# Stack loads over four rounds, output weights in five loads, packing from GpSimd's queue

## The chip, the cores and the metric

The kernel runs on one core of one Trainium2 chip. The metric is the device time of one execution in microseconds; the figure given is the median of several runs. A profile is one further execution, recorded by the hardware profiler.

## The reference

Four layers follow each other on `x` (2048 tokens, 576 features): A, B, A, B, each with a layer norm in front and a residual around it. A is attention with a sliding window of 256 and 32 heads of 18 features; B filters in the frequency domain.

```
def A(x):                       # D = 576, H = 32, Dh = 18, W = 256
    q, k, v = split(x @ wqkv)
    scores = q @ k.T * Dh ** -0.5, masked to 0 <= i - j < W
    return merge(softmax(scores) @ v) @ wo
def B(x):                       # two dimensions, tokens and features
    return irfft2(rfft2(x) * (w_r + 1j * w_i))
x = x + A(layernorm(x)); x = x + B(layernorm(x))
x = x + A(layernorm(x)); x = x + B(layernorm(x))
```

## The kernel before

`prompt_kernel` builds two pairs of an attention layer (`layer_a`) and a spectral layer (`layer_b`); the output projection of the attention, the class `Out`, lies between them. The change touches the attention's main part and `Out`.

**Heads, chunks and rounds.** The 32 heads are worked on in `NQ` = 8 groups of four. A group's sequence is 16 tiles of 128 tokens, in four chunks of 512. The running number x = 16 n + i counts tiles over all groups, 128 in all; a *round* is one x. A round has four score products of each of two kinds, one for each head (`pair`, `hp`):

- `score_max` (L1168, tile S) multiplies queries by keys, and VectorE takes the row maximum (L1170, m). It runs `LEAD` = 10 rounds ahead of the second kind.
- `exps` (L1205, tile E) multiplies keys by queries and a row that holds the negated maximum, so that ScalarE's exponential (L1206, tile P) comes out already shifted. GpSimd sets what lies outside the window to zero (L1208, L1211).
- `part` (L1225, tile U) multiplies P by the values.

**From projection to stacks.** `proj` (L1107) multiplies the normalized tokens by the query and key weights; its result is split in a high and a low part (sg) and stored in DRAM (qk_d, L1128). The low part of later blocks is made by GpSimd (L1125). `stack_load(n, c)` (L1143) fetches chunk c of group n from there into the tiles qs and ks, stacked over partitions as high and low parts: for q and k, for hp 0 and 1, three transfers each, twelve in all, of 72 KB. `qs` and `ks_` have two buffers each, used by groups in turn. `v_load` (L1149 or L1151) fetches a group's values (vq).

**The maxima.** `m_rows(n, c)` turns the maxima of a chunk (L1181), ScalarE negates them (L1183, tile mt), and four transfers of 2 KB (L1188, qs<-mt) write them to the last row of each stack. E of a chunk's tiles needs them; a tile's queries reach two tiles further, so E needs chunk c (c over 0) two rounds before that chunk's own first round.

**Attended values.** After the last `part` of a chunk in burst k, VectorE turns U (L1230), then come `divide` (L1241, L1242) at k + 1, `back` (L1246, tile o) at k + 3 and `store` (L1251, op_d<-o) at k + 4. When a group's four chunks are stored, four calls of `pack(n, h)` (L1258, o_d<-op_d) copy the 18 used rows of 32 of each head from one DRAM tensor to another, in steps 2 bursts apart.

**Order.** The order is written out by hand. `opening` runs the first ten rounds of S. `bursts` then takes three E and three S at a time (a burst is 0.75 round), with products of the projection (up to round 103 or so), parts, and the `steps` put down for that burst. `loads(t)` is called at the start of each round, `behind(t)` at its end. The last ten rounds (`MIX` = 118 on) follow in a loop of their own with two steps a round. Each engine, and each queue that issues transfers (SP, ACT's, POOL's), works in program order; a transfer on SP that waits holds what stands behind it on SP.

**Out.** `room()` runs at round OB - 16 = 104 and asks for the raw output weights (L742) in two transfers; `split(k)` (L749, L750) makes the high and low parts of a fifth of them at rounds 110, 112 to 118. `const` (L756, dc), `load_x` (L764) and `attended` (L772, L775: o_d into oraw) fetch what the output projection (L800, tile ops) and the next layer need. `turn` (L785) and `split_last` (L794) prepare the attended values.

Some copies between DRAM tensors (L1404, dcr<-in_dc and gcr<-in_gc) are issued on GpSimd's queue in the first attention; three pieces of a stack load go there in the opening.

Of the kernel before, what the change touches and what calls it, by code (L numbers as in the profile page):

```python
# [18 lines left out]
NT = 16  # L19
# [622 lines left out]
NQ = 8  # L642
# [73 lines left out]
class Out:  # L716
# [7 lines left out]
    def room(self):  # L724
        self.rh = rh = self.bp.tile([128, 5 * S], F32R, tag="xh", name="oroom")
        self.rl = f = self.bp.tile([128, 4 * S], F32, tag="xl", name="ofree")
        X = 2 * self.n
        self.w = {"h": rh[:, 0:5 * X], "l": rh[:, 5 * X:10 * X]}
        self.oT = [rh[:, 5800 + 896 * k:6696 + 896 * k] for k in range(3)]
        self.oL = [rh[:, 8488 + 256 * k:8744 + 256 * k] for k in range(3)]  # L730
        self.gc = rh[:, 9256:9768].rearrange("p (a j c) -> p a j c", a=2, j=2)
        small = f[:, 8130:8170]
        self.st = [small[:, 12 * k:12 * k + 12] for k in range(2)]
        self.mv = [small[:, 24 + 2 * k:26 + 2 * k] for k in range(4)]
        self.rs = [small[:, 32 + k:33 + k] for k in range(4)]
        self.junk, self.junk2 = f[:, 6804:7092], f[:, 7092:7380]
        self.raw = f[:, 0:5 * X]
        self.x = [f[:, X * k:X * k + X] for k in range(5)]

        self.o7 = f[:, 4756:6804]  # L740
        for a, b in ((0, 2), (2, 5)):
            self.nc.sync.dma_start(self.raw[:, a * X:b * X], self.wo_d[:, a * X:b * X])  # L742

    def xt(self, u):
        return self.x[(u + 4) % 5]
# [118 lines left out]
def layer_a(tc, ident, eps, bp, big, src, dst, wqk_d, wv_d, wo_d, dc_d, gc_d, dram, copy, wvs, second, spectral, share):  # L864

    nc = tc.nc
    V, A, T, P = nc.vector, nc.scalar, nc.tensor, nc.gpsimd
# [14 lines left out]
    if True:  # L882
# [191 lines left out]
        with ExitStack() as c2:  # L1074
# [56 lines left out]

            vts = {}

            def stack_load(n, c):

                q, k = qs[n % 2], ks_[n % 2]
                cs = slice(c * 512, c * 512 + 512)
                for which, t, parts in ((0, q, (0, 0, 1)), (1, k, (0, 1, 0))):
                    for hp in range(2):
                        r0 = 144 * n + 72 * which + 36 * hp  # L1140
                        for slot, part in enumerate(parts):
                            b = 64 * hp + 18 * slot
                            (P if which and (n == 0 and c > 1 or n == 1 and c == 0) else nc.sync).dma_start(  # L1143
                                t[b:b + 18, :, cs].bitcast(F32), qk_d[part, r0:r0 + 36, cs].rearrange("(f d) t -> d f t", f=2).bitcast(F32))

            def v_load(n):
                v = wp.tile([128, NT, 4, 19], F32, tag="vq", name=f"vq{n}", bufs=2)
                if second:
                    nc.sync.dma_start(v.rearrange("p b h e -> p b (h e)"), v_d[n].rearrange("(b p) e -> p b e", p=128))  # L1149
                else:  # L1150
                    nc.sync.dma_start(v.rearrange("p b h e -> p (b h e)"), v_d[n].rearrange("p b e -> p (b e)"))  # L1151
                vts[n] = v
# [102 lines left out]

            def pack(n, h):
                a, b = [f.rearrange("e c x -> (e c x)").rearrange("(a b) -> a b", a=16) for f in (o_d[72 * n + 18 * h:72 * n + 18 * h + 18], op_d[n, 32 * h:32 * h + 18])]
                nc.sync.dma_start(a, b)  # L1258

            for k, (i, c) in enumerate(((0, 0), (1, 0), (0, 1), (1, 1), (0, 2), (0, 3), (1, 2), (1, 3))):  # L1260
                for f in proj(i, c, k % 2):
                    f()
                remainders()

                for b in (32, 96):
                    P.memset(ks_[i][b:b + 32, :, 512 * c:512 * c + 512].bitcast(F32), 1.0)
                    P.memset(qs[i][b:b + 32, :, 512 * c:512 * c + 512].bitcast(F32), 0.0)
                if k in (2, 4):
                    stack_load(0, k // 2 - 1)
# [7 lines left out]
            def loads(t):  # L1277
                if t + LEAD in (0, 2):
                    stack_load(0, 2 + (t + LEAD) // 2)
                if t in (-4, 4, 8, 12):  # L1280
                    stack_load(1, max(t, 0) // 4)
                n, c = divmod(t + 20, NT)
                if c % 4 == 0 and 1 < n < NQ:
                    stack_load(n, c // 4)
                if t + LEAD == 5:
                    v_load(0)
                if t + 12 in range(NT, NX, NT):
                    v_load((t + 12) // NT)
# [18 lines left out]
            steps = {}  # L1307

            def later(k, n, c):
                for lag, f in zip(later.lags, (divide, back, store)):  # L1310
                    steps.setdefault(k + lag, []).append((f, n, c))
                if c == 3:
                    for h in range(4):
                        steps.setdefault(k + (8 + 2 * h if n < NQ - 2 else 7 + h // 2), []).append((pack, n, h))

            later.lags = 1, 3, 4

# [10 lines left out]
            def bursts():  # L1328
# [8 lines left out]
                for k in range(-(-len(es) // 3)):  # L1337
                    e, c = es[3 * k:3 * k + 3], ss[3 * k:3 * k + 3]
                    for x, pair, hp in e:
                        if pair == hp == 0:  # L1340
                            loads(x)
                            assert not any(source(p) == x - 6 for p in parts)
# [9 lines left out]
                    while parts and (took < 430 or source(parts[0]) < e[0][0] - 3 if spread else took == 0 or parts[0][0] % 2 or parts[0][1]):  # L1352
                        if (4 * source(parts[0] if spread else (parts[0][0] | 1, 1)) + 3) // 3 + 2 > k:
                            break
                        x, half = parts[0]
                        if took and half == 0 and (x % 4 == 0 or x % NT == 1):
                            break
                        parts.pop(0)
                        part(x, half)
                        took += lasting((x, half))  # L1360
                        if half and x % 4 == 3:
                            later(k, *divmod(x // 4, 4))
# [24 lines left out]
                    for x, pair, hp in e:  # L1387
                        if pair == hp == 1:
                            behind(x)
                remainders()  # L1390
                assert at == len(pj)
                for p in parts:
                    part(*p)
                    if p[1] and p[0] % 4 == 3:
                        later(k, *divmod(p[0] // 4, 4))

            OB = NX - 8
            out = Out(nc, eps, bp, big, o_d, srcv, dstv, wo_d, dc_d, gc_d, second)

            def behind(t):  # L1400
                if copy and t >= 32 and t % 4 == 0 and t < 32 + 16 * len(copy):

                    z, r = divmod(t // 4 - 8, 4)
                    P.dma_start(*[a[32 * r:32 * r + 32] for a in copy[z]])  # L1404
                if t == OB - 16:
                    out.room()
                if 0 <= t - (OB - 10) < 10 and t % 2 == 0:
                    out.split((t - (OB - 10)) // 2)
                if t - OB + 13 in range(0, 10, 2):
                    out.const((t - OB + 13) // 2)  # L1410
                if t == OB - 3:
                    out.filters()
                if t - OB + 8 in range(0, 10, 2):
                    out.load_x(((t - OB + 8) // 2 + 1) % 5)
                if 0 <= t - (OB - 8) < 6:
                    out.attended(*divmod(t - (OB - 8), 2))
                if t - OB in (1, 2):
                    out.attended(3, t - OB - 1)
                if t == OB + 4:
                    out.ahead_of_last()  # L1420
                if t - OB - 5 in (0, 1, 2):
                    out.turn(t - OB - 5, V)
                if t == NX:

                    A.activation(wp.tile([128, 1], F32, name="se", bufs=1), eps, AF.Sqrt)
# [14 lines left out]
            for t in range(MIX, NX + 2):  # L1440
                loads(t)
                for pair in range(2):
                    for hp in range(2):
                        if t < NX:
                            exps(t, pair, hp)
                    for f, *a in steps.pop(now, ()):
                        f(*a)
                    if pair == 0 and t - 2 < NX:
                        pv(t - 2)
                        if t % 4 == 1 and t - 2 < NX - 4:  # L1450
                            later(now, *divmod(t // 4 - 1, 4))
                    now += 1
                for f, *a in due[:1]:
                    f(*a)
                    due.pop(0)
                behind(t)
# [65 lines left out]
```

## Time and profile before

| | |
|---|---|
| median of 3 runs | 1370.67 us (1363.26 to 1371.69) |
| the profiled execution's own time | 1368.36 us |
| its span, first to last instruction | 1366.3 us |
| mean granted clock of TensorE | 0.988 |
| TensorE busy | 1312.9 us (96%) |
| VectorE, ScalarE, GpSimd busy | 948.7 us (69%), 754.9 us (55%), 696.1 us (51%) |
| bytes moved by DMA | 274.23 MB, 201 GB/s in the mean |

The two attentions' bursts lie at about 128 to 479 us and 829 to 1178 us of the span. In the rows, PE is TensorE's matmuls, PEld its weight loads, DVE VectorE, ACT ScalarE, POOL GpSimd, SP the queue of SyncE; a q behind a name means the sequencer that issues transfers. `out<-in` are the names of tiles. A row of a timeline gives start, duration, engine, line and operation, and in brackets the engine's idle time before it and what ended that. A group's row gives its count, busy time, mean ns of one, and idle time before it with the releasers.

### The profile page before, as it was taken

How to read it: one execution, taken by the hardware profiler on the slowest of the kernel's cores; microseconds unless marked ns; L12 is line 12 of the kernel's file. 1: busy time of each engine (PE TensorE's matmuls, PEld its weight loads, DVE VectorE, ACT ScalarE, POOL GpSimd, SP SyncE). 2: the span in 40 equal slices, each digit the busy share in tenths (PEclk: the TensorE clock that was granted, in tenths of full speed). 3: DMA queues.
4: the chain of work that ended last, by engine and by line, in shares of the span. 5: the costliest groups of instructions: out<-in, count | busy, mean ns of one | idle time of the engine just before them, and what ended most of it. 6: DMA issues, size and time to landing. Idle time of an engine off the chain costs nothing.

```text
span 1366.3 us, 33335 instructions
## 1 busy us (share of the span) xinstructions
PE 1312.9 (96%) x10911; PEld 964.4 (71%) x10911; DVE 948.7 (69%) x3132; ACT 754.9 (55%) x1896; POOL 696.1 (51%) x1156
## 2 busy tenths in 40 slices
PE   9999999899998899999999999999999998999998
PEld 8986666566655499985899975556556654699588
DVE  5418888788887577757674148888788878476755
ACT  5622776577766735443355315677667767575233
POOL 2257666566655634567221295566556657212731
PEclk9999999999999999999999999999999999999999
DMA  6756665666556827678883367566556568488875
GB/s 204 210 165 204 201 200 178 196 189 181 180 173 201 242 78 245 194 244 266 275 264 74 99 202 210 183 183 182 178 176 174 181 173 280 132 288 298 300 246 178
DMA packets 179392, 274.23 MB, mean 201 GB/s; under 512 B 68415, under 2 KB 78399, under 8 KB 177893
## 3 DMA queue, kind: packets, MB, share of 16 engines
q1 hardware_dynamic: 168399, 250.71, 59.4%
q10 hardware_dynamic: 7702, 15.03, 3.1%
q0 software_dynamic: 3120, 6.36, 1.8%
q8 instruction: 88, 1.44, 0.4%
q14 instruction: 83, 0.68, 0.2%
HBM read 164.54 MB, written 114.81 MB: 204 GB/s over the span
## 4 chain that ended last, share of the span: by engine, by line
PE 84%; DMA 7%; DVE 3%; ACT 3%; issue 2%; POOL 1%; SPq 1%; ACTq 0%; DVEq 0%; POOLq 0%
PE pj L1107 19%; PE S L1168 12%; PE U L1225 11%; PE vps L1003 9%; PE ops L800 6%; PE E L1205 6%; DMA qs<-mt 4%; PE po L274 4%; PE pq L524 3%; PE p L503 2%; PE pf L274 2%; PE pi L600 2%; PE pz L312 1%; ACT P L1206 1%; DMA dc<-dcr 1%
## 5 line engine op out<-in xcount | busy, mean ns | idle before, releaser
L1170 DVE CUSTOM_DVE_ANT_0 jk<-S,mask 128x384 bf16<-128x384 f32 (+2 forms) x1024 | 490.0, 526 | 102.7 <-PE S L1168 59.8
L1206 ACT ACTIVATE P<-E 128x384 f32<-128x384 f32 (+2 forms) x1024 | 409.4, 475 | 206.7 <-PE E L1205 172.8
L1168 PE MATMUL S<-ks,qs 63*128 63x384 f32 (+2 forms) x1024 | 282.8, 378 | 2.0 <-DVE m L1170 0.8
L1208 POOL TENSOR_SCALAR_AFFINE_SELECT P<-P 128x512 f32<-128x512 f32 x256 | 163.8, 640 | 235.5 <-ACT P L1206 227.1
L1205 PE MATMUL E<-qs,ks 64*128 64x384 f32 (+2 forms) x1024 | 236.0, 381 | 29.0 <-DMA qs<-mt 22.2
L1168 PEld LDWEIGHTS S<-ks,qs 63*128 63x128 f32 x1024 | 147.0, 187 | 116.5 <-DVE m L1170 81.5
L1225 PE MATMUL U<-P,vq 128*19 128x128 f32 (+1 forms) x3840 | 193.2, 334 | 3.3 <-DVE us L1230 2.2
L1205 PEld LDWEIGHTS E<-qs,ks 64*128 64x128 f32 x1024 | 121.0, 189 | 51.8 <-ACT P L1206 23.4
L1107 PE MATMUL pj<-xh,wqh 128*128 128x512 f32 x360 | 156.3, 434 | 0.4 <-DVE sg L1125 0.2
L1225 PEld LDWEIGHTS U<-P,vq 128*19 128x19 f32 x3840 | 96.7, 99 | 84.5 <-issue 22.4
L1211 POOL TENSOR_SCALAR_AFFINE_SELECT P<-P 128x512 f32<-128x512 f32 x224 | 143.0, 638 | 0.0
L1107 PE MATMUL pj<-xh,wql 128*128 128x512 f32 x360 | 122.9, 418 | 0.0
L1107 PE MATMUL pj<-xl,wqh 128*128 128x512 f32 x288 | 120.1, 417 | 0.0
L800 PE MATMUL ops<-oroom 128*128 128x290 f32 (+1 forms) x812 | 114.0, 297 | 1.7 <-DVE ofree L846 1.3
L800 PEld LDWEIGHTS ops<-oroom 128*128 128x128 f32 x812 | 110.4, 189 | 2.3 <-ACT ofree L834 1.5
L1107 PEld LDWEIGHTS pj<-xh,wqh 128*128 128x128 f32 x360 | 68.0, 189 | 32.5 <-issue 14.4
L1170 DVE DVE_READ_ACCUMULATOR2_ANT m<- 128x1 f32 x1024 | 84.9, 83 | 0.0
L1119 ACT CAST sg<-pj 128x512 fp32r<-128x512 f32 x72 | 42.3, 588 | 70.7 <-PE pj L1107 62.2
L1107 PEld LDWEIGHTS pj<-xh,wql 128*128 128x128 f32 x360 | 64.5, 189 | 21.9 <-issue 10.9
L1230 DVE STREAM_TRANSPOSE us<-U 128x512 f32<-128x512 f32 x64 | 45.8, 716 | 46.4 <-PE U L1225 46.4
L1107 PEld LDWEIGHTS pj<-xl,wqh 128*128 128x128 f32 x288 | 54.5, 189 | 16.9 <-issue 9.0
L274 PE MATMUL po<-dc,half 128*128 128x290 f32 x384 | 63.4, 302 | 0.0
(508 smaller groups left out, 2206.9 us busy)
## 6 DMA issues: line engine op xcount, KB each, us to landing
qk_d<-sg SPq DMA_DIRECT2D x56, 512.0 KB
qs<-qk_d SPq DMA_DIRECT2D x384, 72.0 KB
ks<-qk_d SPq DMA_DIRECT2D x348, 72.0 KB
op_d<-o SPq DMA_DIRECT2D x56, 256.0 KB
v_d<-vt SPq DMA_DIRECT2D x32, 304.0 KB
vq<-v_d SPq DMA_DIRECT2D x16, 608.0 KB
wt<-in_w SPq DMA_DIRECT2D x16, 580.0 KB
ofree<-x SPq DMA_DIRECT2D x16, 580.0 KB
```

The lines of the kernel that those rows point to most:

```text
L274: T.matmul(ps[:, c, 0:NF], tail[r] if si == 4 else hl_(si), dcs[b // 2][r, b % 2], start=mi == si == 0, stop=si == 4)
L800: self.nc.tensor.matmul(self.ps[u][n][:, 0:self.n], x, self.w[p][:, (2 * wk + n) * self.n:(2 * wk + n + 1) * self.n], start=first and i == ...
L1003: T.matmul(ps[:, n, 0:288], xT(xk, c), w[:, wk, n * 288:(n + 1) * 288], start=i == 0, stop=i == len(ks) - 1)
L1107: T.matmul(box["ps"].rearrange("r (n p) -> r n p", n=NT) if second else box["ps"], w[:, wk], x, start=s == 0, stop=s == len(ks) - 1)
L1168: T.matmul(ps[:, 0:N], q[b:b + 63, pair, i * 128:i * 128 + 128], k[b:b + 63, pair, lo:hi], start=True, stop=True)
L1170: V.tensor_tensor_reduce(out=jk[:, 0:N], in0=ps[:, 0:N], in1=mask[:, 384 - N:384], scale=1.0, scalar=-3e38, op0=ALU.add, op1=ALU.max, accu ...
L1205: T.matmul(ps[:, 0:nq], k[b:b + 64, pair, j * 128:j * 128 + 128], q[b:b + 64, pair, j * 128:j * 128 + nq], start=True, stop=True)
L1206: A.activation(p[:, hl_, 0:nq], ps[:, 0:nq], AF.Exp, scale=SC)
L1208: P.affine_select(out=p[:, :, 0:128], in_=p[:, :, 0:128], pattern=[[0, 4], [1, 128]], compare_op=ALU.is_ge, fill=0.0, base=0, channel_mult ...
L1211: P.affine_select(out=p[:, :, 256:384], in_=p[:, :, 256:384], pattern=[[0, 4], [-1, 128]], compare_op=ALU.is_gt, fill=0.0, base=0, channel ...
L1225: T.matmul(U[32 * h:32 * h + 19, (q0 % 4) * 128:(q0 % 4) * 128 + 128 * (q1 - q0)], vts[n][:, j, h], pt[n, j][:, h, (q0 - j) * 128:(q1 - j) ...
L1230: V.transpose(u, U.rearrange("r (p n) -> r n p", n=NT))
```

## The change

Three things change.

- A chunk's twelve transfers are asked for in four rounds, three in each: q for hp 0, q for hp 1, k for hp 0, k for hp 1. They begin in the round in which all twelve stood before. In rounds 12 to 15 the last chunk of group 1 and the first of group 2 are loaded side by side. The first chunk of group 1 (round -4) and group 0 stay as they were.
- The raw output weights come in five transfers, one for each `split`, at rounds 104, 106 to 112.
- `pack` is issued on GpSimd's queue in place of SP, and two steps later: at k + 10, 12, 14, 16 in place of k + 8, 10, 12, 14, and for the last of these groups at k + 9, 9, 10, 10 in place of k + 7, 7, 8, 8.

```diff
@@ class Out, room
         self.o7 = f[:, 4756:6804]
-        for a, b in ((0, 2), (2, 5)):
-            self.nc.sync.dma_start(self.raw[:, a * X:b * X], self.wo_d[:, a * X:b * X])
+
+    def weights(self, k):
+        c = slice(2 * self.n * k, 2 * self.n * (k + 1))
+        self.nc.sync.dma_start(self.raw[:, c], self.wo_d[:, c])
@@ stack_load
-            def stack_load(n, c):
+            def stack_load(n, c, some=range(4)):
 
                 q, k = qs[n % 2], ks_[n % 2]
                 cs = slice(c * 512, c * 512 + 512)
                 for which, t, parts in ((0, q, (0, 0, 1)), (1, k, (0, 1, 0))):
                     for hp in range(2):
+                        if 2 * which + hp not in some:
+                            continue
                         r0 = 144 * n + 72 * which + 36 * hp
@@ pack
-                nc.sync.dma_start(a, b)
+                P.dma_start(a, b)
@@ loads
-                if t in (-4, 4, 8, 12):
-                    stack_load(1, max(t, 0) // 4)
-                n, c = divmod(t + 20, NT)
-                if c % 4 == 0 and 1 < n < NQ:
-                    stack_load(n, c // 4)
+                if t == -4:
+                    stack_load(1, 0)
+                n, c = divmod(t + (12 if t < 16 else 20), NT)
+                if 4 <= t < 16 or 1 < n < NQ and t >= 12:
+                    stack_load(1 if t < 16 else n, t // 4 if t < 16 else c // 4, (t % 4,))
+                if 12 <= t < 16:
+                    stack_load(2, 0, (t % 4,))
@@ later
-                        steps.setdefault(k + (8 + 2 * h if n < NQ - 2 else 7 + h // 2), []).append((pack, n, h))
+                        steps.setdefault(k + (10 + 2 * h if n < NQ - 2 else 9 + h // 2), []).append((pack, n, h))
@@ behind
                 if t == OB - 16:
                     out.room()
+                if t - OB + 16 in range(0, 10, 2):
+                    out.weights((t - OB + 16) // 2)
```

## The prediction

> **What bounds the kernel now.** I read the page first, its busy shares and its chain by line, then the costliest groups.
>
> ```profile
> PE 1312.9 (96%) x10911; PEld 964.4 (71%) x10911; DVE 948.7 (69%) x3132; ACT 754.9 (55%) x1896; POOL 696.1 (51%) x1156
> PE pj L1107 19%; PE S L1168 12%; PE U L1225 11%; PE vps L1003 9%; PE ops L800 6%; PE E L1205 6%; DMA qs<-mt 4%; PE po L274 4%; PE pq L524 3%; PE p L503 2%; PE pf L274 2%; PE pi L600 2%; PE pz L312 1%; ACT P L1206 1%; DMA dc<-dcr 1%
> L1205 PE MATMUL E<-qs,ks 64*128 64x384 f32 (+2 forms) x1024 | 236.0, 381 | 29.0 <-DMA qs<-mt 22.2
> ```
>
> TensorE is busy for 1312.9 of 1366.3 us, so whatever is to be won lies in its 53 us of idle time and in its clock. The largest item with one name is qs<-mt: the small transfers of the negated row maxima (L1188), for which E (L1205) stands idle 22.2 us. They are issued on SP, the queue that the change relieves.
>
> What would a stretch without such waits cost? The view by windows compares two stretches of the first attention that do the same work, sixteen rounds each: the first has none of these waits, the second has the one of the third line.
>
> ```profile
> 306.90:349.40 42.50, 42.31 (x424) 25.93 (x426) 35.71 (x138) 29.43 (x74) 25.28 (x38) 1.00 0.60 181
> 213.70:261.80 48.10, 46.28 (x430) 28.06 (x426) 37.10 (x145) 30.31 (x77) 29.71 (x44) 0.96 0.65 200
> ...
> 244.39 1.14 PE L1205 MATMUL E<-qs,ks 64*128 64x384 f32 x3 [1.79 <-DMA qs<-mt]
> ```
>
> Columns of the first two: stretch, its us, then busy us of PE, PEld, DVE, ACT and POOL, granted clock, DMA. The first shows what is left when no maxima are late: 42.5 us with TensorE busy 42.3, so nothing else stands ready to take the wait's place there. The second is 5.6 us longer, with a wait of 1.8 us and a clock of 0.96. In the whole trace six stretches run near half clock, beside such waits; first, last and sum:
>
> ```profile
> 244.30:247.70 3.40, 3.31 (x10) 1.98 (x10) 1.21 (x5) 1.59 (x4) 0.58 (x1) 0.54 0.43 129
> ...
> 1162.50:1169.30 6.80, 6.64 (x54) 2.94 (x58) 0.00 (x0) 3.63 (x9) 1.40 (x3) 0.52 0.51 143
> sum 30.60, PE 28.90 PEld 14.92 DVE 8.91 ACT 13.03 POOL 8.24; mean PE 4.82 PEld 2.49 DVE 1.49 ACT 2.17 POOL 1.37
> ```
>
> Why are the maxima late? SP's timeline at the worst wait among the bursts, with ScalarE's and TensorE's rows:
>
> ```profile
> 959.60 0.27 ACT L1183 ACTIVATE mt<-tpm 16x128 fp32r<-16x128 f32 x1 [0.42 <-PE tpm L1181]
> 957.70 0.53 SPq L1258 DMA_DIRECT2D o_d<-op_d  x1
> ...
> 958.95 2.44 SPq L1143 DMA_DIRECT2D qs<-qk_d  x6
> 961.44 4.05 SPq L1143 DMA_DIRECT2D ks<-qk_d  x6
> 965.53 0.84 SPq L1258 DMA_DIRECT2D o_d<-op_d  x1
> ...
> 967.09 2.56 SPq L1188 DMA_DIRECT2D qs<-mt  x4
> 969.28 0.41 PE L1205 MATMUL E<-qs,ks 64*128 64x384 f32 x1 [2.76 <-DMA qs<-mt]
> ```
>
> The maxima are ready at 959.87 and leave at 967.09. In those 7.2 us SP works off one stack load, twelve issues in 6.5 us, and one pack. E at 969.28 has waited 2.76 us. So the bound is SP's order, not the transfer: from first issue to E's start it takes 2.2 us.
>
> SP itself stands still too. In the view of waits (who waited for what: us in total, times, longest), E first, then SP:
>
> ```profile
> PE E L1205 <- DMA qs<-mt: 22.2, 13, 3.4
> ...
> SPq L1143 <- DMA qk_d<-sg: 60.7, 35, 9.5
> SPq L1143 <- DMA qs<-qk_d: 32.1, 63, 2.6
> SPq L1258 <- DMA op_d<-o: 20.2, 10, 3.4
> ```
>
> The third line is issues of one stack load that wait for earlier ones to land; the last is the pack at the head of SP, waiting for the store that it reads.
>
> **Part 1, the stack pieces.** Nothing is removed: a chunk still takes 12 issues, now three in each of four rounds. In program order the maxima of chunk c come about 1.3 rounds before the next chunk's first pieces, and the store of the attended values about one round after them. Before, the twelve stand ahead of both. Now six stand ahead of the store, at most six more between store and maxima. Twelve take 4.9 us or more (the 364.77 rows below: 2.14 + 2.73, 0.36 us each at least), so the maxima meet a queue shorter by 2.2 us at least, and by what of the 32.1 us of mutual waits the smaller groups avoid. A wait of 2.76 us with 7.2 us of lag needs 2.8 us. The price is that a chunk's last pieces are asked for three rounds (3 x 42.5/16 = 8 us) later. S (L1168) reads chunks ten rounds ahead of E, and seven rounds, 18.6 us, remain. For head group 1 the load starts only six rounds ahead of its reader, so three rounds are left, and from round 12 to 15 two loads run at once, six issues a round, 2.2 of 2.7 us. There I expect S to wait 1 us or so per attention: 2 us in all; bounds 0 and 6 us (three chunks, 1 us each, two attentions).
>
> **Part 2, packs on POOL.** SP loses 56 issues of 0.53 us, 30 us, and the 20.2 us of waiting. POOL gains the issues. Their nearest row is a copy between DRAM tensors issued from POOL in the same rounds:
>
> ```profile
> L1404 POOL DMA_DIRECT2D dcr<-in_dc x4: 557/572/590, 218.2 to 254.9; - x4
> L1208 POOL TENSOR_SCALAR_AFFINE_SELECT P<-P 128x512 f32<-128x512 f32 x256 | 163.8, 640 | 235.5 <-ACT P L1206 227.1
> L1225 PE MATMUL U<-P,vq 128*19 128x128 f32 (+1 forms) x3840 | 193.2, 334 | 3.3 <-DVE us L1230 2.2
> 372.73 0.64 POOL L1211 TENSOR_SCALAR_AFFINE_SELECT P<-P 128x512 f32<-128x512 f32 x1
> 375.14 1.50 PE L1225 MATMUL U<-P,vq 128*19 128x256 f32 x32
> ```
>
> That is 56 x 0.57 = 32 us on an engine that waits 227 us for ScalarE's exponentials at its masks (L1208). The cover: POOL's last mask ends at 373.37, and the U that could read it starts at 375.14, 1.8 us later; TensorE stands 3.3 us in all before U. So 0.57 us at a time costs nothing; without that cover it would be the whole 32 us.
>
> The change adds a wait on POOL: the first pack of a group waits for the landing of the fourth store, and masks and the remainders of the projections queue behind it. How late is that store?
>
> ```profile
> 361.33 0.71 DVE L1246 STREAM_TRANSPOSE o<-us 128x512 f32<-128x512 f32 x1
> 364.77 2.14 SPq L1143 DMA_DIRECT2D qs<-qk_d  x6
> 366.96 2.73 SPq L1143 DMA_DIRECT2D ks<-qk_d  x6
> 369.78 0.34 SPq L1151 DMA_DIRECT2D vq<-v_d  x1
> 370.22 0.38 SPq L1251 DMA_DIRECT2D op_d<-o  x1
> 377.43 0.53 SPq L1258 DMA_DIRECT2D o_d<-op_d  x1
> ```
>
> Its data are ready at 362.04; it leaves at 370.22, behind twelve stack issues, and the pack follows on its landing at 377.4. With six pieces fewer it leaves 2.2 us earlier, and the packs come two bursts later (a burst is 0.75 round, 2.0 us), 4 us. The longest such wait on SP was 3.4 us, less than 6.2. I take 0. The other bound is that nothing is gained: 14 first packs x (3.4 - 1.8) = 22 us.
>
> **Part 3, the weights, and the end of the attention.**
>
> ```profile
> 429.73 0.86 SPq L742 DMA_DIRECT2D ofree<-in_wo  x2
> 431.22 7.37 DMA qs<-mt
> 438.72 1.03 PE L1205 MATMUL E<-qs,ks 64*128 64x384 f32 x2 [1.55 <-DMA qs<-mt]
> 452.38 0.56 SPq L1251 DMA_DIRECT2D op_d<-o  x1
> 457.01 0.25 ACT L1183 ACTIVATE mt<-tpm 16x128 fp32r<-16x128 f32 x1
> 459.20 1.74 SPq L1258 DMA_DIRECT2D o_d<-op_d  x2
> 461.05 2.88 SPq L1188 DMA_DIRECT2D qs<-mt  x4
> 463.56 1.25 PE L1205 MATMUL E<-qs,ks 64*128 64x384 f32 x2 [2.23 <-DMA qs<-mt]
> 469.40 3.28 SPq L775 DMA_DIRECT2D oraw<-o_d  x4
> ```
>
> The line with 7.37 is from the chain. These maxima take so long because 1.44 MB of weights was asked for just ahead; in five loads, two of 288 KB are. Three more issues of 0.43 us per layer fall on a queue that has lost more. Each load still comes six rounds, over 12 us, before its split. The last maxima are ready at 457.26 and held until 461.05 by a pack that waits for the store of 452.38. Off SP, they leave 3.8 us earlier, and E's 2.23 us go. These packs are now two rounds later; the loads that read them (L775) were issued from 469.4 on, so they stay hidden.
>
> **The sum**, against the profiled execution's 1368.4 us (its span is 1366.3):
> - E's waits: 22.2 us. I keep 4 us for places where large loads still lie ahead of the maxima: -18.
> - Clock: of 30.6 us at half clock, the three stretches of 3.4 us and one of 6.8 us lie where TensorE is the limit; half of 17 is 8.5. The other two lie at an attention's end, where ScalarE limits: 0.5 each. -9.5. Next late after that is TensorE itself, as in the 42.5 us stretch.
> - Late pieces +2, POOL 0.
>
> 1368.4 - 18 - 9.5 + 2 = 1343. The median shown is 1370.7, 2.3 us above that execution; I name 1343 and leave this in the range.
>
> The Trainium skill (TensorE: Matmul & The Clock Gate, What's actually happening) lets the clock drop after an idle window of about 3.4 us. Of E's 13 waits the longest is 3.4 us and the one beside the first slow stretch 1.8, so the trace is stricter than the page; by the page the clock term would stay and the sum be 1352.
>
> **Rivals.**
> 1. *Half.* SP runs ahead of the rounds as far as its waits let it, so the pieces spread in program order may still bunch, and the 60.7 us for qk_d, true dependences, stay. Then packs and weights alone act: the two ends (2.2 + 3.4 + 1), the 1.55 us at 438.72 with its clock 1.7, and perhaps 4 more: 14, 1355. For it: late head groups load what was projected just before. Against: at 958.95 the twelve are held up by nothing but themselves. Chance 0.18.
> 2. *POOL gives it back.* The store lands as late as before: +22 on 1343 is 1365, no change. Against: the 6.2 us above. 0.10.
> 3. *Slower: issuing on POOL costs more than the cover.* If a pack holds POOL w us, U is late by w - 1.8 each; 56 (w - 1.8) exceeds the 25 us gained from w = 2.25 us on, and at 2.8 us gives 1343 + 56 = 1399. Against: 0.56 to 0.59 us in all eight copies at L1404, with VectorE 84% busy (35.71 of 42.5). 0.06. The Trainium skill (SBUF — State Buffer, SBUF: two separate sides) says that VectorE operations on two ports lock GpSimd out of writing descriptors; its figure, 0.62 us growing to 3.1 us, would as an estimate make 1343 + 73 = 1416. The L1404 rows speak against it here.
>
> **The numbers.** The forecast, 1330 to 1352, has 0.66. Low end: all waits, all of the clock term at 15.3 and no late pieces give 1331, a little more if SP's other stalls shrink: 1329. High end: half the gain, 1355, and a median 2.3 higher with a few us for the late pieces' upper bound: 1361. What remains outside is rivals 2 and 3 and little else. Repeats of this kernel differ by 8 us, and about 1% is what a measurement of it can tell from no change: faster by over that (below 1357) is the forecast and most of rival 1, 0.78; within it, rival 2 and the rest of 1, 0.16; slower 0.06.
>
> **What the next profile would show.** E's idle before L1205 under 8 us; half-clock stretches two or fewer; the maxima leaving within 2 us of ScalarE's row; packs on POOL at 0.57 us with no wait; no growth of the idle before U and at most 2 us before S. I am wrong if SP's maxima still trail by 3 us, if POOL shows waits on op_d, or if S waits for ks.

## The result and the profile after

The changed kernel takes 1361.99 us (median of 17 runs; the kernel before 1369.47 in the same 17): ratio 0.9935, 95% interval 0.9916 to 0.9955. Two of its 17 runs, the profiled one among them, ran slow (1955 and 5379 us, clock 0.56 and 0.21), and the ratio leaves them out. The changed kernel is faster, by 9 us by the ratio; 28 were forecast, and 1361.99 lies 1 us above the range. Two repeats gave 0.9940 (0.9916 to 0.9963) and 0.9942 (0.9912 to 0.9972). The profile after is that of the second repeat, called g1 below, whose own time is 1362.4 us; the span is 1360.3 and the mean clock 0.983. Lines have moved: S is now L1172, E L1209, the maxima L1192, the stack loads L1147, the projection's stores L1130, the packs L1262.

g1: busy time, then the groups of E and S.

```profile
PE 1312.2 (96%) x10911; PEld 964.4 (71%) x10911; DVE 950.0 (70%) x3132; ACT 753.7 (55%) x1896; POOL 721.8 (53%) x1212
L1209 PE MATMUL E<-qs,ks 64*128 64x384 f32 (+2 forms) x1024 | 232.8, 380 | 18.4 <-DMA qs<-mt 12.5 <-ACT P L1210 5.5
L1172 PE MATMUL S<-ks,qs 63*128 63x384 f32 (+2 forms) x1024 | 281.2, 376 | 5.8 <-DMA ks<-qk_d 4.8
```

TensorE is as busy as before (1312.9 us), so the whole gain is idle time: 53.4 us became 48.1. E waits 12.5 us for maxima, 9.7 less than before. S, which waited for nothing that matters, now waits 4.8 us for late pieces. Waits of E for ScalarE fell from 6.5 to 5.5. That is -9.7 + 4.8 - 1.0 = -5.9, and the two profiled executions differ by 6.0 (1368.4 to 1362.4). That the sum closes so well is partly luck: from the first E to the last U the two attentions together are 9.2 us shorter (699.9 to 690.7), and the rest of the span is 3.2 us longer (666.4 to 669.6).

View of waits of g1 (who waited for what: us in total, times, longest):

```profile
PE E L1209 <- DMA qs<-mt: 12.5, 8, 4.1
PE S L1172 <- DMA ks<-qk_d: 4.8, 4, 1.7
SPq L1147 <- DMA qk_d<-sg: 57.7, 22, 10.0
SPq L1147 <- DMA qs<-qk_d: 19.7, 28, 2.9
SPq L1130 <- POOL sg L1127: 13.4, 11, 2.7
```

SP's wait at the packs is gone, and the issues of a stack load wait less for each other (32.1 to 19.7). The last line was 1.4 us before: with the packs off SP, it stands at the projection's stores, for GpSimd's half of the data. The prediction never mentioned this wait.

Packs on GpSimd in g1 (the second row is its sequencer's waits ahead of them: ns minimum, median, maximum):

```profile
L1262 POOL DMA_DIRECT2D o_d<-op_d x56: 496/534/587, 202.5 to 1155.1; - x56
L1262 POOLq EVENT_SEMAPHORE  x28: 17/43/2036, 200.1 to 1149.9; - x28
```

They cost what the sum said, 0.53 us each, and nothing ahead of U grew.

The clock did not recover. g1 by windows, two of its eight half-clock stretches inside the attentions (a third follows a wait of S at 855.73), and the sum of the eight; ahead of them TensorE's rows at two places:

```profile
178.78 0.41 PE L1172 MATMUL S<-ks,qs 63*128 63x384 f32 x1 [1.49 <-DMA ks<-qk_d]
879.45 0.41 PE L1172 MATMUL S<-ks,qs 63*128 63x384 f32 x1 [1.66 <-DMA ks<-qk_d]
```

```profile
180.20:183.60 3.40, 3.40 (x20) 1.79 (x21) 1.85 (x10) 1.84 (x6) 1.26 (x2) 0.56 0.78 258
...
880.30:883.70 3.40, 3.40 (x11) 2.21 (x12) 1.28 (x7) 1.31 (x4) 0.81 (x2) 0.50 0.77 266
...
sum 40.10, PE 36.21 PEld 18.68 DVE 18.36 ACT 17.80 POOL 15.97; mean PE 4.53 PEld 2.33 DVE 2.29 ACT 2.22 POOL 2.00
```

In these places a wait of S of about 1.5 us is followed, about 1 us later, by 3.4 us at half clock in which TensorE is busy throughout: about 1.7 us more. So a late piece can cost twice, but needn't: in e1, the same kernel, S waits 2.04 us at 871.14 and no half clock follows. Nor is it particular to S: in g2, where no piece is late, E's wait of 2.03 us at 179.60 has the same stretch behind it. Before, 30.6 us ran at half clock in the attentions, in g1 40.1, in the profile of e1 30.6; over all runs the mean clock is 0.985 before (30 runs) and 0.985 after (7 and 6 runs).

### The profile page after: what moved, and what is told of

It reads as the page before. It is cut to its first block, busy times and chain, and to the rows that moved or that the text cites. A ratio compares the mean times of both kernels' runs of the same rounds, so it can differ in the third digit from the quotient of the medians.

```text
span 1952.9 us, 33382 instructions
## 1 busy us (share of the span) xinstructions
PE 1938.2 (99%) x10911; PEld 1237.2 (63%) x10911; DVE 980.7 (50%) x3132; ACT 764.7 (39%) x1896; POOL 723.6 (37%) x1212
## 4 chain that ended last, share of the span: by engine, by line
PE 97%; DMA 1%; issue 1%; ACT 0%; DVE 0%; SPq 0%; DVEq 0%; ACTq 0%
PE pj L1109 21%; PE U L1229 14%; PE S L1172 12%; PE vps L1005 10%; PE ops L802 9%; PE po L274 5%; PE E L1209 5%; PE pq L524 3%; PE p L503 3%; PE pi L600 3%; PE pf L274 2%; PE pz L312 2%; PE wo L274 1%; PE warm L376 1%; PE tpaa L710 1%; PE tpm L1185 1%
## 5 line engine op out<-in xcount | busy, mean ns | idle before, releaser
L1172 PE MATMUL S<-ks,qs 63*128 63x384 f32 (+2 forms) x1024 | 319.6, 471 | 0.0
L1229 PE MATMUL U<-P,vq 128*19 128x128 f32 (+1 forms) x3840 | 295.1, 467 | 3.0 <-DVE us L1234 3.0
L1172 PEld LDWEIGHTS S<-ks,qs 63*128 63x128 f32 x1024 | 149.3, 222 | 191.3 <-DVE m L1174 90.6
L1209 PE MATMUL E<-qs,ks 64*128 64x384 f32 (+2 forms) x1024 | 252.0, 436 | 5.2 <-ACT P L1210 3.6
L1109 PE MATMUL pj<-xh,wqh 128*128 128x512 f32 x360 | 211.4, 587 | 0.0
L802 PE MATMUL ops<-oroom 128*128 128x290 f32 (+1 forms) x812 | 181.6, 405 | 0.0
L1109 PE MATMUL pj<-xh,wql 128*128 128x512 f32 x360 | 177.0, 580 | 0.0
L802 PEld LDWEIGHTS ops<-oroom 128*128 128x128 f32 x812 | 162.5, 216 | 14.2
L1109 PE MATMUL pj<-xl,wqh 128*128 128x512 f32 x288 | 165.0, 573 | 0.0
L1209 PEld LDWEIGHTS E<-qs,ks 64*128 64x128 f32 x1024 | 126.6, 229 | 18.1 <-ACT P L1210 7.7
L274 PE MATMUL po<-dc,half 128*128 128x290 f32 x384 | 99.7, 418 | 0.0
L1005 PE MATMUL vps<-wv,xh 128*128 128x288 f32 x320 | 86.4, 416 | 0.0
L1005 PE MATMUL vps<-half,xh 128*128 128x288 f32 x320 | 86.2, 414 | 0.0
```

The lines of the kernel that those rows point to most:

```text
L274: T.matmul(ps[:, c, 0:NF], tail[r] if si == 4 else hl_(si), dcs[b // 2][r, b % 2], start=mi == si == 0, stop=si == 4)
L802: self.nc.tensor.matmul(self.ps[u][n][:, 0:self.n], x, self.w[p][:, (2 * wk + n) * self.n:(2 * wk + n + 1) * self.n], start=first and i == ...
L1005: T.matmul(ps[:, n, 0:288], xT(xk, c), w[:, wk, n * 288:(n + 1) * 288], start=i == 0, stop=i == len(ks) - 1)
L1109: T.matmul(box["ps"].rearrange("r (n p) -> r n p", n=NT) if second else box["ps"], w[:, wk], x, start=s == 0, stop=s == len(ks) - 1)
L1172: T.matmul(ps[:, 0:N], q[b:b + 63, pair, i * 128:i * 128 + 128], k[b:b + 63, pair, lo:hi], start=True, stop=True)
L1209: T.matmul(ps[:, 0:nq], k[b:b + 64, pair, j * 128:j * 128 + 128], q[b:b + 64, pair, j * 128:j * 128 + nq], start=True, stop=True)
```

## The experiments

Sixteen runs were made, of fourteen kernels; "before" beside them had a median of 1369.8 to 1370.9. E and S are TensorE's waits for maxima and for stack pieces in the profile, in us; the clock is the mean over the runs.

| | kernel | median us | ratio, 95% | clock | E | S |
|---|---|---|---|---|---|---|
| e1 | whole change | 1363.5 | 0.9940 [0.9916, 0.9963] | 0.985 | 11.4 | 4.4 |
| e2 | spread alone | 1379.2 | 1.0071 [1.0050, 1.0093] | 0.981 | 24.9 | 6.6 |
| e3 | weights alone | 1368.9 | 0.9992 [0.9970, 1.0013] | 0.983 | 23.5 | 0.4 |
| e4 | packs alone | 1364.9 | 0.9966 [0.9941, 0.9991] | 0.984 | 18.5 | 1.1 |
| f1 | packs, weights | 1353.9 | 0.9898 [0.9866, 0.9930] | 0.989 | 10.3 | 0.4 |
| f2 | spread from round 16 on | 1358.5 | 0.9917 [0.9889, 0.9946] | 0.987 | 13.6 | 0 |
| f3 | before, no maxima sent | 1333.4 | 0.9731 [0.9702, 0.9761] | 0.997 | 0 | 0 |
| f4 | whole change, maxima on ScalarE's queue | 1532.4 | 1.1180 [1.1149, 1.1212] | 0.935 | 0 | 21.2 |
| g1 | whole change | 1362.6 | 0.9942 [0.9912, 0.9972] | 0.985 | 12.5 | 4.8 |
| g2 | as f1 | 1356.4 | 0.9906 [0.9878, 0.9934] | 0.987 | 9.7 | 0 |
| g3 | g2, chunks whole, 2 rounds later | 1373.7 | 1.0017 [0.9986, 1.0047] | 0.984 | 21.7 | 0 |
| g4 | g2, projection's stores on GpSimd | 1344.5 | 0.9815 [0.9789, 0.9842] | 0.992 | 8.7 | 0 |
| h1 | whole change, stores on GpSimd | 1347.5 | 0.9829 [0.9792, 0.9865] | 0.990 | 4.1 | 3.1 |
| h2 | before, stores on GpSimd | 1363.6 | 0.9954 [0.9926, 0.9982] | 0.985 | 13.4 | 0 |
| h3 | g4, packs not two steps later | 1354.4 | 0.9885 [0.9847, 0.9922] | 0.990 | 5.0 | 0 |
| h4 | g4, weights in two loads | 1346.4 | 0.9834 [0.9796, 0.9871] | 0.991 | 5.8 | 0.5 |

E and S come from one execution each, which can lie well off the median: e3's is 8.0 us above it, h3's 5.0 and f2's 4.0 above, g3's 7.7 below.

**The parts alone (e1 to e4).** Each of e2 to e4 takes one part of the diff into the kernel before: `stack_load` with `loads`; `weights`; `pack` with its two steps.

> The change as a whole, once more, with a profile at the full clock. Known: 0.9935 of the time before, about 9 us, where 27 were forecast. Theory A (the waits for the maxima are gone, the clock term stays): E waits under 8 us for qs<-mt, granted clock 0.985 to 0.990 as before, more than four stretches at half clock, now without a wait for the maxima beside them. Rival B (late pieces): S waits 10 us or more for ks or qs pieces. Rival C (half): E still waits 10 us or more for qs<-mt and SP issues the maxima over 2 us after ScalarE wrote them.

> Only the stack pieces over four rounds; weights in two loads and packs on SP as before. Theory A: E's waits for qs<-mt fall from 22 us to about 12 (the two attention ends and the rounds with packs stay), time 3 to 6 us below before. Rival B: S waits as long as in the whole change, time equal to before or above it. Rival C: no change of E's waits, time within 2 us of before.

> Only the output weights in five loads. Theory A and B: E's wait at the first round of the last group (1.55 us in the first attention) goes, time 0 to 3 us below before. Rival C, that large loads ahead of the maxima are most of the loss: 4 us or more below before.

> Only the packs on GpSimd's queue and two steps later. Theory A: the waits at both attention ends (2.2 and 3.4 us) go and the lag of the maxima on SP shrinks by 1 to 2 us; E's waits for qs<-mt 10 to 13 us, time 5 to 9 us below before. Rival B: more than the whole change gains, 10 us or more below before, since no piece is late. A rival for POOL: packs wait for the store and masks come late, idle before U grows from 3.3 us to over 8.

e1 went as its rival C had it: E still waits 11.4 us, and the maxima leave 2.5 us after ScalarE's row in the mean. e4 gained 5 us, but E kept 18.5 us where 10 to 13 were expected. The spread, which the sum credited with most of the gain, makes the kernel 0.7% slower by itself. SP's timeline of e2 at E's longest wait (L742 weights, L1145 stack, L1190 maxima, L1260 pack; the maxima were ready at 427.75), then SP's waits that belong to it:

```profile
432.05 0.87 SPq L742 DMA_DIRECT2D ofree<-in_wo  x2
432.97 1.09 SPq L1145 DMA_DIRECT2D qs<-qk_d  x3
434.10 1.77 SPq L1145 DMA_DIRECT2D ks<-qk_d  x3
438.07 0.47 SPq L1260 DMA_DIRECT2D o_d<-op_d  x1
440.99 1.00 SPq L1145 DMA_DIRECT2D ks<-qk_d  x3
442.11 2.54 SPq L1190 DMA_DIRECT2D qs<-mt  x4
444.92 1.02 PE L1207 MATMUL E<-qs,ks 64*128 64x384 f32 x2 [5.62 <-DMA qs<-mt]
```

```profile
SPq L1145 <- DMA ofree<-in_wo: 2.4, 1, 2.4
SPq L1260 <- DMA ofree<-in_wo: 2.2, 1, 2.2
```

The pack at 438.07 and the pieces at 440.99 need nothing of the weights, and still each starts when one of the two large loads of 432.05 has landed: each is the eighth issue after the one that it waits for. Before, the chunk's twelve stood ahead of these loads; spread, nine stand behind them, and the maxima behind the nine, 14 us late. So the spread and the two large loads act on each other, and in g1, with five smaller loads, SP's waits at stack pieces and packs for the weights are 1.3 us in place of 4.6. The parts' own differences, +0.71, -0.08 and -0.34%, add to +0.3%; together they give -0.6%. A sum of parts can't hold that.

**With and without the spread (f1, g2), and the early rounds (f2).** f1 and g2 are the same kernel: the changed one with `loads` and `stack_load` of before. f2 keeps the spread from round 16 on.

```diff
-                if 4 <= t < 16 or 1 < n < NQ and t >= 12:
-                    stack_load(1 if t < 16 else n, t // 4 if t < 16 else c // 4, (t % 4,))
...
+                if t in (-4, 4, 8, 12):
+                    stack_load(1, max(t, 0) // 4)
+                n, c = divmod(t + 20, NT)
+                if t == 12:
+                    stack_load(2, 0)
+                if 1 < n < NQ and t >= 16:
+                    stack_load(n, c // 4, (t % 4,))
```

> Packs on GpSimd and weights in five as in the changed kernel, the twelve stack issues again in one round. Theory (the spread moves six or more issues from behind the last maxima, where SP has time, to behind the store of the next projection, where the maxima come next): S's two waits of 2.4 and 2.0 us at rounds 16 to 20 go, the maxima in the middle groups leave within 1 us more often than in the changed kernel, and at round 112 they trail by 3 us in place of 9; the time is 1357 to 1363 us, not above the changed kernel's 1363.5. Rival (once packs are off SP the spread is worth what it was meant for): 1366 us or more, E waits for maxima over 15 us.

> The changed kernel, but the loads of rounds 4 to 15 in one round each as before; the spread begins at round 16. Theory (late pieces cost what TensorE shows before S, 4.4 us, and about 1.5 us of clock behind it): no wait of S for qs or ks over 0.3 us, first 24 rounds shorter by 2 us in each attention, 1357.5 to 1360 us. Rival (the wait only changes its name, as the maxima of round 18 come behind twelve issues): E at round 18 waits 1 us or more and the time stays at 1362 to 1365 us.

> The changed kernel once more, on the same chip as the next one: 1359 to 1366 us.

> Once more packs and weights without the spread. Theory (the spread costs): 1351 to 1358 us, at least 4 us below the changed kernel beside it. Rival (the two differ only by the chip and the run): within 2 us of it.

Without the spread the kernel takes 1353.9 and 1356.4 us, 9.6 and 6.1 us less than with it by the medians (e1 and f1 on two chips, g1 and g2 on one), 6.6 and 4.9 by the means, each with a standard error of 2. f1 came out below what was expected, g2 as expected. f2, 1358.5, lies between; its interval overlaps those of both neighbours. In f1 the maxima at round 112 trail by 3.15 us, as expected, but in g2 by 5.45.

Where E waits shows where the spread costs. SP sends the maxima of 60 chunks; the lag is from the end of ScalarE's row to SP's first issue. Round 112 is the first chunk of the last group, once in each attention, and E's waits are split at the moment when its maxima are ready. All in us, from one profile each; the lag in the first column is a mean over the chunks before round 112.

| | kernel | lag before | lag at round 112 | E before | E from then on | S |
|---|---|---|---|---|---|---|
| | before | 3.3 | 5.1, 4.4 | 14.9 | 7.2 | 0 |
| e2 | spread alone | 3.2 | 14.4, 14.0 | 8.5 | 16.4 | 6.6 |
| f1 | packs, weights | 2.4 | 3.2, 3.8 | 7.2 | 3.1 | 0.4 |
| g2 | as f1 | 2.6 | 5.5, 3.0 | 7.4 | 2.2 | 0 |
| e1 | whole change | 2.2 | 9.0, 9.0 | 1.6 | 9.8 | 4.4 |
| g1 | whole change | 2.0 | 9.3, 7.7 | 1.6 | 10.9 | 4.8 |
| f2 | spread from round 16 on | 2.3 | 7.5, 6.7 | 5.5 | 8.1 | 0 |

Up to the last group the spread does a part of what it was meant for: E waits about 6 us less there in each pair, though the lag is shorter by 0.6 us at most in the mean. But 2.0 (f1) and 3.8 us (g2) of this stood at round 18, where now S waits for late pieces instead. f2 shows the exchange, as its rival had it: S waits for nothing, and E waits at round 18 again. Its time is the theory's all the same.

```profile
182.28 0.96 PE L1209 MATMUL E<-qs,ks 64*128 64x384 f32 x3 [1.54 <-DMA qs<-mt]
874.20 0.89 PE L1209 MATMUL E<-qs,ks 64*128 64x384 f32 x3 [1.82 <-DMA qs<-mt]
```

From the last group on, E waits 7 to 9 us more with the spread than without it. How pieces get ahead of the maxima is plainest in the middle of an attention, at the first chunk of group 4, though E waits for nothing there. ScalarE's row and SP's timeline, first g1, then g2 (there L1145 stack, L1253 store, L1130 projection's store, L1190 maxima):

```profile
290.10 0.26 ACT L1187 ACTIVATE mt<-tpm 16x128 fp32r<-16x128 f32 x1
287.06 1.05 SPq L1147 DMA_DIRECT2D qs<-qk_d  x3
288.21 0.35 SPq L1255 DMA_DIRECT2D op_d<-o  x1
288.61 1.15 SPq L1147 DMA_DIRECT2D qs<-qk_d  x3
290.04 0.39 SPq L1130 DMA_DIRECT2D qk_d<-sg  x1
290.47 4.21 SPq L1147 DMA_DIRECT2D ks<-qk_d  x6
294.78 1.73 SPq L1192 DMA_DIRECT2D qs<-mt  x2
```

```profile
291.66 0.25 ACT L1185 ACTIVATE mt<-tpm 16x128 fp32r<-16x128 f32 x1
287.38 2.29 SPq L1145 DMA_DIRECT2D qs<-qk_d  x6
289.71 2.54 SPq L1145 DMA_DIRECT2D ks<-qk_d  x6
292.56 0.34 SPq L1253 DMA_DIRECT2D op_d<-o  x1
293.01 0.39 SPq L1130 DMA_DIRECT2D qk_d<-sg  x1
293.56 2.90 SPq L1190 DMA_DIRECT2D qs<-mt  x3
```

In g2 the twelve issues follow the last maxima at once and are over by 292.25; SP then meets the two stores and sends the maxima 1.65 us after ScalarE's row ends. In g1 six pieces stand behind both stores, go out when the maxima are ready, and hold them 4.42 us. Here SP issued the twelve in time that it had, and the spread moved half of them behind SP's waits, next to the maxima. That is one place and not the rule: pieces go out between ScalarE's row and the maxima at 41 of the 60 chunks before, at 35 in g2 and at 40 in g1. At round 112, where E needs the maxima, all twelve stand behind the wait for the projection's last store in both kernels, with a store and a weights load beside them: in g1 the pieces of four rounds have gathered there, and the same fourteen issues are ahead of the maxima as without the spread. In g2 these fourteen take 7.0 us (416.63 to 423.67) and begin 1.7 us before the maxima are ready; in g1 they take 9.1 and begin when the maxima are ready:

```profile
417.57 0.27 ACT L1187 ACTIVATE mt<-tpm 16x128 fp32r<-16x128 f32 x1 [0.78 <-PE tpm L1185]
414.28 0.39 SPq L1130 DMA_DIRECT2D qk_d<-sg  x1
417.92 2.16 SPq L1147 DMA_DIRECT2D qs<-qk_d  x3
...
421.05 1.15 SPq L1147 DMA_DIRECT2D qs<-qk_d  x3
422.24 4.82 SPq L1147 DMA_DIRECT2D ks<-qk_d  x6
427.18 2.44 SPq L1192 DMA_DIRECT2D qs<-mt  x4
430.79 1.03 PE L1209 MATMUL E<-qs,ks 64*128 64x384 f32 x2 [2.92 <-DMA qs<-mt]
```

The later waits are explained only in part. Those for the attention's last chunk, behind which no stack load is left, are 6.5 us in g1 and 3.9 in e1, 3.0 and 1.9 in f1 and g2. No run takes the spread out of the last group alone.

**What the maxima can cost at most (f3), and another queue for them (f4).** f3 is the kernel before without the four transfers in `m_rows`; f4 is the changed kernel with them on ScalarE's queue.

```diff
-                        (nc.sync if n or c > 1 else nc.scalar).dma_start(q[b:b + 1, ...
+                        nc.scalar.dma_start(q[b:b + 1, ...
```

> The kernel before without the transfers of the row maxima: the row in the stacks stays at zero, so the exponentials are not shifted; everything else runs. It bounds the first two terms of my sum together. If the 22.2 us of E's waits are worth their length and the half-clock stretches hang on them (my sum): 1370 - 22 - 10 to 15 = 1333 to 1338 us and clock over 0.993. If the clock has other causes: 1345 to 1350 us with the clock at 0.986 to 0.989. If other waits take the place of E's (ScalarE, S, U): 1355 us or more.

> The changed kernel with all maxima issued on ScalarE's queue, right behind the row that makes them. If SP's order is what still holds them: lag under 0.7 us everywhere, E's waits for maxima under 3 us, and if ScalarE can give the time, 11 us less, 1352 us. The price is 240 issues of 0.58 us, 139 us, on a ScalarE that is 69% busy in these stretches, at 2.4 us a time in front of exponentials: if that is on the path, E or U wait for ScalarE instead, about 1 us in each of 64 places or more, 1365 to 1400 us.

f3, the group of E:

```profile
L1199 PE MATMUL E<-qs,ks 64*128 64x384 f32 (+2 forms) x1024 | 224.6, 373 | 4.4 <-ACT P L1200 4.3
```

1333.4 is the first of the three expectations: E's waits are worth their 22 us, most of the half-clock stretches hang on them (mean clock 0.997; three of 3.4 us are left at the attentions' ends), and nothing else takes their place. The bound that the prediction named was the right one, and its worth, 37 us, too.

f4 is far slower. ScalarE's timeline and TensorE's waits:

```profile
301.00 0.25 ACT L1187 ACTIVATE mt<-tpm 16x128 fp32r<-16x128 f32 x1
301.27 2.44 ACTq L1192 DMA_DIRECT2D qs<-mt  x4
303.76 2.41 ACT L1210 ACTIVATE P<-E 128x384 f32<-128x384 f32 x6 [2.52 <-DMA qs<-mt]
```

```profile
PE E L1209 <- ACT P L1210: 68.7, 66, 2.8
```

The maxima leave at once, and the exponentials stand still for 2.5 us each time. 60 places more than in the changed kernel at 2.5 us are 150 us; the kernel lost 169, and 1532 lies far above the 1365 to 1400 expected. What S's waits of 21.2 us and the clock of 0.935 have in this isn't taken apart. ScalarE is 55% busy over the span in the changed kernel, and it had nothing to give at these places.

**Place or splitting (g3), and the wait that holds the pieces (g4, h1, h2).** g3 is g2 with whole chunks, two rounds later from round 16 on (the first chunk of group 2 stays at round 12). g4 is g2 with the projection's stores on GpSimd, which makes the second half of their data; h1 and h2 do the same to the changed kernel and to the one before.

```diff
# g3
-                n, c = divmod(t + 20, NT)
+                n, c = divmod(t + 18, NT)
...
# g4, h1, h2
-                            (nc.scalar if i < 2 else nc.sync).dma_start(qk_d[...
+                            (nc.scalar if i < 2 else P if aside else nc.sync).dma_start(qk_d[...
```

> The kernel of g2 with each chunk from round 16 on whole, but asked for two rounds later, so that its twelve issues stand just ahead of the maxima as most of the spread pieces do. If place decides: the maxima of groups 3 to 6 leave 3 us or more behind ScalarE's row, E waits 14 to 22 us for them, 1358 to 1368 us. If splitting itself costs (more, smaller groups of issues): like g2, 1351 to 1358 us, lag as there.

> The kernel of g2 with the projection's stores from the point on where GpSimd makes the low part (L1130) issued on GpSimd's queue: one more wait of SP, for ScalarE and GpSimd, leaves the maxima's way. If what remains of E's waits is SP's order: E under 6 us, 1343 to 1350 us (the kernel without maxima took 1333). If true dependences of late groups hold SP anyway: E as in g2, 1351 to 1358 us. If 42 more issues of 0.57 us on GpSimd are on the path: U waits 10 us more, 1360 us or more.

> The changed kernel, spread and all, with the projection's stores on GpSimd's queue as in g4. If the spread costs because SP waits for a store's data between a chunk's pieces, that wait is gone: 1344 to 1350 us, of which the waits of S (4 to 5 us) are what stands over g4's 1344.5. If it costs because its pieces stand ahead of the maxima at all, as in g3: 1352 to 1358 us, mean lag of the maxima 0.8 us or more over g4's.

> The kernel before with only the projection's stores on GpSimd's queue. If each wait of SP that goes is worth its own part: 1370.5 less the 10 to 12 us between g2 and g4, 1358 to 1361 us. If the packs, which wait for a landing on SP, still hold everything: 1364 us or more.

g3 splits nothing and is 17 us slower than g2 (E 21.7 against 9.7; 5 us more than expected): place alone does it, by more than the spread itself. g4 is 11.9 us faster than g2 and beats both kernels: 1344.5. ScalarE's row and SP's timeline of g4 in the same rounds, and the moved stores (ns, minimum, median, maximum):

```profile
286.60 0.25 ACT L1185 ACTIVATE mt<-tpm 16x128 fp32r<-16x128 f32 x1
277.35 3.87 SPq L1145 DMA_DIRECT2D qs<-qk_d  x6
281.26 3.03 SPq L1145 DMA_DIRECT2D ks<-qk_d  x6
284.40 0.34 SPq L1253 DMA_DIRECT2D op_d<-o  x1
286.87 2.58 SPq L1190 DMA_DIRECT2D qs<-mt  x4
```

```profile
L1130 POOL DMA_DIRECT2D qk_d<-sg x44: 735/774/807, 151.9 to 1097.0; - x44
```

Here SP waits for the maxima, not they for SP: they are ready at 286.85 and leave at 286.87. The 44 stores cost GpSimd 34 us and show in no wait of TensorE's U for it over 0.3 us. The mean lag fell from 2.4 us in g2 to 1.4, and the mean clock rose from 0.987 to 0.992. Where all of the 11.9 us lies isn't shown: E still waits 8.7 us in g4's profile, the slowest of its five executions, where under 6 were expected (5.8 in h4, 4.1 in h1).

With this wait off SP the spread costs 3 us in place of 6 to 10 by the medians (h1 against g4, on two chips; the intervals overlap), which can't be told from nothing. E waits 4.1 us in place of 8.7, S 3.1 in place of 0, and the mean lag is 1.0 in place of 1.4. This fits the first of h1's expectations: the harm came in the main by way of SP's wait at these stores; with it gone, the spread does shorten E's waits. h2 shows again that the parts don't simply add: alone on the kernel before, with packs still on SP, the same edit brings 6 us, between its two expectations.

**The two terms that no run had isolated (h3, h4).** h3 undoes the two steps of `pack` in g4, h4 the five loads.

> The kernel of g4 with the packs as early as before (two steps earlier). It asks what the two steps were worth. If the store leaves early enough anyway: 1343 to 1347 us, GpSimd's waits for op_d under 5 us. If GpSimd now stands as SP stood (20.2 us in 10 waits, up to 3.4) with masks behind it: U and E later, 1350 to 1360 us.

> The kernel of g4 with the output weights in two loads again. My sum gave them the 1.55 us at round 112 with its clock, in each attention: 1346.5 to 1349 us, and the maxima of group 7's first chunk land 8 us after their issue. If they are worth nothing: 1343 to 1346 us.

```profile
PE U L1227 <- POOL P L1210: 12.4, 9, 3.0
L1260 POOLq EVENT_SEMAPHORE  x28: 17/43/6125, 195.0 to 1146.4; - x28
```

These two lines are h3's: at the old steps GpSimd waits up to 6.1 us for landings, masks queue behind, and U waits 12.4 us: 1354.4, 10 us more than g4. The wait of 3.4 us on SP was no measure of it. With the stores on GpSimd's queue too, as here, the two steps carry the second part. The five loads are worth 1.9 us by the medians of g4 and h4, at the lower edge of the first expectation, and 0.08% in e3; neither can be told from nothing.

## Why the prediction missed, step by step

- **The bound** (E's waits for maxima, held by SP's order, with the clock): right, and shown by f3 at the forecast size, 37 us.
- **"The maxima meet a queue shorter by 2.2 us at least"**: this is the step that failed. Up to the last group the lag shortened by 0.2 to 0.6 us in the mean (e1, g1 against f1, g2), and S's waits for late pieces took back most of what E gained. At the last group the queue is longer by 4 to 6 us: the pieces of four rounds gather behind SP's wait for the projection's last store, the maxima leave 7.7 to 9.3 us after ScalarE's row in place of 3.0 to 5.5, and E waits 9.8 and 10.9 us from there on in place of 3.1 and 2.2. The step counted issues ahead of the maxima in program order, and one store between them, not the projection's; it didn't ask where SP stands waiting among them. It took the one worst burst, where SP was late already from the chunk before, for the rule: 7.2 us of lag, where the mean before is 3.3. (Twelve issues can also take less than its 4.9 us: 4.4 at 410.64 in the profile before.) It was put at a gain and is a loss of about 5 us by the means, 6 to 10 by the medians (g1 and e1 against g2 and f1).
- **E's waits, -18 to leave 4**: -9.7, 12.5 left, 10.9 of it from the last group on. Without the spread 9.7 to 10.3 are left, over 7 of it before the last group, and 4.1 with spread and the projection's stores off SP (h1). I had kept 4 us for places behind large loads, and taken the attentions' ends as solved with the packs.
- **Late pieces, +2 (0 to 6)**: 4.4 and 4.8 in the two profiles, over the 2 that went into the sum and inside the bounds; the half-clock stretches behind them, three in g1 (about 5 us) and one in e1, were not in the sum.
- **Clock, -9.5**: 0. The assumption that it hangs on the waits is right in the main (0.997 in f3), but new waits of S and the larger ones left at rounds 112 and 122 took the place of the old. The rule of the Trainium skill that I had set against this term (TensorE: Matmul & The Clock Gate, What's actually happening), an idle window of about 3.4 us, is not what the rows show: waits of 1.5 and 1.7 us are followed by half clock, and not each of that length is (2.04 us in e1, 2.76 at 969.28 before).
- **Packs on GpSimd, 0**: right, at 0.53 us each; h3 shows that, beside the moved stores, it holds only with the two later steps. The third rival didn't come: neither these nor the 44 stores of g4 grew beside VectorE.
- **Weights**: E now starts 3.6 us after the issue of the maxima of round 112 (427.18 to 430.79) and not 7.5, but they leave 9.3 us after ScalarE's row, so the 1.55 us there became 2.92. By the runs the five loads alone are worth nothing that can be told. Beside the spread they may keep its worst case away (14 us of lag in e2, 9 in g1), but e2 has its packs on SP too, and no run changes the loads alone there.
- **Rivals**: the first, *Half*, named the mechanism ("the pieces spread in program order may still bunch") and its 1355 is what packs and weights give alone (1353.9, 1356.4). It took the bunched spread to cost nothing. That it costs is the case I had not written down.

## What to carry to other kernels

Issues on an in-order queue cost nothing while the queue would stand idle, and their full length once they stand behind a wait that ends as late as what follows them. So don't count what lies ahead of an urgent transfer in program order; ask at which waits the queue stands between two urgent transfers and what comes behind the last of them. Put bulk issues right after the urgent one, and move transfers that wait to a queue with nothing urgent behind them, a store to the engine that makes its data, far enough behind that it doesn't wait either: here packs and stores together were worth 25 us (g4), where a finer grain alone lost 10 (e2).

## What the runs showed of the hardware

A wait of TensorE of 1.5 us was at times enough for 3.4 us at half clock, in which it was busy all the time (g1 at 178.78 and 879.45), and one of 2.04 us at times not (e1 at 871.14). In this program the transfers of SP use eight semaphores in turn, and in e2 a pack and a stack piece, each the eighth issue after a large load, waited over 2 us for the landing of loads that they had nothing to do with. Four small transfers issued by ScalarE held it for 2.44 us, about as long as SP needs for them, and the exponentials behind them stood still for 2.52; of f4's span 7%, 107 us, lie at these issues on the chain that ended last. A store from on-chip memory took GpSimd 0.77 us to issue where SP took 0.38. The Trainium skill (DMA: Bandwidth & Descriptors, Rules for kernel authors) says that spreading transfers over issuing engines saves only sequencer issue time. The bandwidth half of that no run here tests; the saved issue time of g4's 44 stores would by SP's 0.38 us be 17 us on a queue with time to spare, and with the stores SP's waiting for their data left too (6.5 us in g2); the runs don't tell the two apart.
